# Attention's product of masked weights with values, computed in two halves of the array's columns

## The chip, the cores and the metric

The kernel runs on one core of one Trainium2 chip. The metric is the device time of one execution in microseconds (us), the median of several runs. One execution was also recorded by the hardware profiler; every row below is of that execution.

The core has a matrix engine (TensorE, PE in rows; its weight loads are listed apart as PEld), a vector engine (VectorE, DVE), a scalar engine (ScalarE, ACT), GpSimd (POOL) and SyncE (SP), which starts DMA transfers. A product on TensorE first loads one operand, the weights, into the 128 x 128 array, then streams the other operand, the moving columns, through it; the result lands in PSUM, one partition for each weight column.

## The reference

The program is an mLSTM attention followed by two mixture layers.

```
# attention, for every batch b (4), head h (8), step t (768), head width 40
C = f_stab * C + i_stab * outer(v_t, k_t)
n = f_stab * n + i_stab * k_t
y_t = sigmoid(o_t) * (C @ q_t) / max(|n . q_t|, 1)
# first layer: x is y with heads side by side, 3072 rows x 320
x = prelu(x @ w_in, alpha) @ w_out            # 320 -> 2048 -> 320
# second layer: each row goes to the one expert of 8 with the largest logit
out[row] = gate[row] * (relu(x[row] @ w1[e]) @ w2[e])
```

## The kernel before

The recurrence is computed in blocks of 128 steps. There are U = 24 units, one for each batch and block of 128 steps, and each unit does all 8 heads. For one unit:

- `att_s` (L762): scores of keys against queries, tiles `ps`. The contraction has only 40 rows, so two heads stand at once in the array, one on its rows 0 to 39 and one on rows 64 to 103.
- `att_e` and `att_m` (L752, L753, L770): the decay matrix `D` (steps by steps, one for each head) is loaded, exponentiated on ScalarE, masked on GpSimd, and multiplied with the scores on VectorE. D then holds the masked weights.
- `att_b` (L858): the product of D with the values, tile `pa`. For each head the weights are the 128 x 128 matrix D, the moving operand is 41 columns (40 of the values and one of ones, which gives the denominator). The products of 8 heads land side by side in one PSUM bank.
- `att_h`, `att_n`, `att_a` (L784, L805, L874): the part that comes from the state carried over from earlier blocks, tile `pb`, added to pa.
- `att_d` (L815), `att_u`, `att_v`: the block's contribution to the state, tile `pd`.
- `att_y` (L883 to L900), `att_c`, `att_x` (L911 to L923): division by the denominator, output gate, transposition (`pt`) into the first layer's input.

The first layer runs on 8 groups of 3 units. For each group and each of 16 slices of the hidden width there is `ffn1` (L934, tile `ph`, 8 products of 384 moving columns), an activation on ScalarE and VectorE (L947 to L956) and `ffn2` (L968 to L971, tiles `acc`, 9 products). The second layer (L326) runs after it, slot by slot. Weights of the first layer are also unpacked at the start (L658 to L662, L674, L691, L699, L712), and the experts' weights are split into two parts and written back to memory beside the first layer (L1206, L1207, L1214, L1215).

The order of all steps of the first part is written out by hand, in a list of step names (`ORDER`); `ab` is `att_b`, `as` is `att_s`, `F` is `ffn1`, `S` is `ffn2`. Each engine runs its instructions in that order. So blocks of attention products stand between the blocks of the first layer on TensorE.

An fp32 product appears in the trace as two rows of loads and two of matmuls; a product of the type fp32r (`ph`, `acc`, L326) as one. The tiles ps, pa, pb, pd, pt and some others share three PSUM banks by turns (`ps_att`).

Of the kernel before, what the change touches and what calls it, by code (L numbers as in the profile page):

```python
# [18 lines left out]
B, H, S, D = 4, 8, 768, 40  # L19
# [199 lines left out]
def mlstm_moe_kernel(  # L219
# [19 lines left out]
    V, A, G, T = nc.vector, nc.scalar, nc.gpsimd, nc.tensor  # L239
# [5 lines left out]
    def ps_att(name):  # L245
        return ps.tile([P, 512], F32, tag="att", bufs=3, name=name)
# [237 lines left out]
    with ExitStack() as p1:  # L484
# [367 lines left out]
        def att_b(u):  # L852
            b, c = divmod(u, NC)
            t = ut[u]
            v1 = t["kv"][:, 360:729]
            pa = ps_att(f"pa_{u}")
            for h in range(H):
                T.matmul(  # L858
                    pa[:, h * 41 : (h + 1) * 41],
                    t["D", h // 4][:, h % 4],  # L860
                    v1[:, h * 41 : (h + 1) * 41],
                    start=True,
                    stop=True,
                )
            t["pa0"] = pa

        def att_a(u):
# [566 lines left out]
```

## Time and profile before

| | |
|---|---|
| median of 3 runs | 764.89 us (762.24 to 766.14) |
| the profiled execution, its own time | 763.64 us |
| its span, first to last instruction | 761.8 us |
| TensorE matmuls, busy | 744.0 us (98%), 4907 rows |
| TensorE weight loads, busy | 711.0 us (93%) |
| VectorE, busy | 464.7 us (61%) |
| ScalarE, busy | 367.1 us (48%) |
| GpSimd, busy | 182.6 us (24%) |
| DMA | 179.38 MB in packets, mean 235 GB/s |

Busy shares are averages over a program with several stages. Matmuls are pipelined and the ends of their rows are modelled, so that neighbouring rows overlap; starts are measured. What a block on TensorE costs is therefore read from the start of its first row to the start of the next block's first row.

### The profile page before, as it was taken

Reading aid. Unit: us, or ns where it says so; the run is one execution under the profiler, and the core shown is the slowest. Engines: PE = TensorE matmul, PEld = TensorE weight load, DVE = VectorE, ACT = ScalarE, POOL = GpSimd, SP = SyncE. Lnnn points to the kernel's source line nnn. Section 1 sums busy time; section 2 is a strip of 40 time slices with the busy share of each in tenths; the row PEclk is TensorE's granted clock in tenths of the full one; section 3 lists DMA queues with packets and bytes.
Section 4 is the critical chain, followed back from the end, with each engine's and each line's share of the span. In section 5 each row is a group of like instructions: output and inputs, shape, how many; then the busy total and the mean of one; then the engine's idle time right before and its main releaser. Section 6 shows DMA issues by size and latency. Waiting matters only on the chain.

```text
span 761.8 us, 15188 instructions
## 1 busy us (share of the span) xinstructions
PE 744.0 (98%) x4907; PEld 711.0 (93%) x4907; DVE 464.7 (61%) x1119; ACT 367.1 (48%) x840; POOL 182.6 (24%) x240
## 2 busy tenths in 40 slices
PE   5999999999999999999999999999999999999997
PEld 5898999999999999999999999998999999999996
DVE  5888997867675576776787785867322232233222
ACT  3746586736655564654655454433333333233322
POOL 2443454423222232200010000013222232222223
PEclk9569999999999999999999999999999999999999
DMA  7876679879787848778787978794968645921100
GB/s 244 268 211 217 193 233 317 258 241 305 263 302 233 284 178 256 229 245 289 264 272 253 292 254 302 262 356 154 419 273 317 235 164 197 426 100 39 39 13 22
DMA packets 81515, 179.38 MB, mean 235 GB/s; under 512 B 8620, under 2 KB 39209, under 8 KB 80156
## 3 DMA queue, kind: packets, MB, share of 16 engines
q1 hardware_dynamic: 77980, 169.66, 65.0%
q0 software_dynamic: 3456, 8.71, 3.4%
q8 instruction: 45, 0.74, 0.4%
q14 instruction: 34, 0.28, 0.1%
HBM read 246.29 MB, written 55.59 MB: 396 GB/s over the span
## 4 chain that ended last, share of the span: by engine, by line
PE 85%; DVE 7%; DMA 2%; ACT 2%; issue 2%; POOL 1%; SPq 0%; POOLq 0%; ACTq 0%; DVEq 0%
PE ph L934 22%; PE po L326 13%; PE p L326 13%; PE acc L968 7%; PE acc L969 7%; PE acc L971 7%; PE pa L858 4%; PE p L424 3%; PE ps L762 3%; PE pb L784 1%; PE pd L815 1%; PE xt L386 1%; PE pt L911 1%; ACT D L752 1%; DMA er<-in_ew_dram 1%
## 5 line engine op out<-in xcount | busy, mean ns | idle before, releaser
L934 PE MATMUL ph<-ring 128*128 128x384 f32 x1024 | 198.3, 342 | 0.1
L934 PEld LDWEIGHTS ph<-ring 128*128 128x128 f32 x1024 | 177.7, 189 | 2.6 <-DVE ring L956 0.8
L968 PE MATMUL acc<-ring 128*128 128x336 f32 x384 | 122.4, 324 | 0.0
L969 PE MATMUL acc<-ring 128*128 128x336 f32 x384 | 119.5, 317 | 0.0
L947 ACT ACTIVATE v<-ph 128x384 f32<-128x384 f32 x128 | 62.4, 489 | 100.9 <-PE ph L934 98.7
L446 DVE TENSOR_SCALAR yo<-po,xg 128x320 f32<-128x320 f32 x26 | 14.3, 551 | 137.5 <-PE po L326 137.5
L326 PE MATMUL po<-ring,hh 128*128 (+1 forms) x432 | 95.6, 308 | 0.0
L949 DVE SCALAR_TENSOR_TENSOR ph<-v,al,ph 128x384 f32<-128x384 f32 x104 | 63.8, 618 | 49.3 <-ACT v L947 48.9
L326 PE MATMUL p<-ring,xh 128*128 (+1 forms) x324 | 89.9, 399 | 0.0
L971 PE MATMUL acc<-ring 128*128 128x336 f32 x384 | 80.1, 316 | 0.0
L326 PEld LDWEIGHTS po<-ring,hh 128*128 128x128 f32 x432 | 73.2, 187 | 2.3 <-ACT hh L426 0.2
L956 DVE TENSOR_TENSOR ring<-ph,ring 128x384 fp32r<-128x384 f32 x104 | 57.4, 554 | 27.0 <-ACT ring L955 26.1
L968 PEld LDWEIGHTS acc<-ring 128*128 128x128 f32 x384 | 72.2, 188 | 0.9
L969 PEld LDWEIGHTS acc<-ring 128*128 128x128 f32 x384 | 72.2, 188 | 0.0
L955 ACT ACTIVATE ring<-ph 128x384 fp32r<-128x384 f32 x104 | 50.6, 488 | 44.1 <-DVE ph L949 38.7
L426 ACT ACTIVATE hh<-p 128x512 fp32r<-128x512 f32 x54 | 29.4, 595 | 86.4 <-PE p L424 86.4
L326 PEld LDWEIGHTS p<-ring,xh 128*128 128x128 f32 x324 | 58.8, 188 | 11.5 <-DMA ring<-scr 0.2
L326 PE MATMUL po<-ring,hl 128*128 (+1 forms) x216 | 66.6, 308 | 0.2 <-DVE hl L428 0.2
L447 POOL DMA_INDIRECT out_dram<-yo,tok x28 | 28.1, 1003 | 160.8 <-DVE yo L446 135.8
L413 ACT ACTIVATE hr<-p 128x512 f32<-128x512 f32 x56 | 33.4, 597 | 67.5 <-PE p L326 65.1
L971 PEld LDWEIGHTS acc<-ring 128*128 128x128 f32 x384 | 63.6, 189 | 0.0
L752 ACT ACTIVATE D<-D,EKT 128x128 f32<-128x128 f32 x192 | 60.2, 393 | 3.5 <-DMA D<-gd 3.3
(211 smaller groups left out, 1180.4 us busy)
## 6 DMA issues: line engine op xcount, KB each, us to landing
ring<-scr SPq DMA_DIRECT2D x26, 3072.0 KB
ring<-scr SPq DMA_DIRECT2D x26, 2560.0 KB
ring<-scr SPq DMA_DIRECT2D x33, 512.0 KB
D<-gd SPq DMA_DIRECT2D x48, 256.0 KB
er<-in_ew_dram SPq DMA_DIRECT2D x32, 384.0 KB
scr<-ring SPq DMA_DIRECT2D x32, 384.0 KB
scr<-er SPq DMA_DIRECT2D x32, 384.0 KB
er<-in_ew_dram SPq DMA_DIRECT2D x32, 320.0 KB
```

The costliest lines, as they stand in the source:

```text
L326: mm = T.matmul(o_, lhsT, r, start=start, stop=stop)
L413: A.activation(hr_half(j, hf), ph, AF.Relu)
L752: A.activation(d[:, j], d[:, j], AF.Exp, bias=EKT[:, c, i + j : i + j + 1])
L858: T.matmul(pa[:, h * 41 : (h + 1) * 41], t["D", h // 4][:, h % 4], v1[:, h * 41 : (h + 1) * 41], start=True, stop=True,)
L934: T.matmul(ph[:, :384], wi_[i][lo][:, wc], xTs[n % 2][:, xc], start=(a == 0), stop=(a == len(PASSES) - 1),)
L947: A.activation(v, ph[:, :384], AF.Relu, scale=-1.0)
L949: V.scalar_tensor_tensor(g, v, al1[:, i : i + 1], ph[:, :384], ALU.mult, ALU.add)
L955: A.activation(gh, v, AF.Copy)
L956: engine(V, G, "ffn_split", k).tensor_tensor(gl, v, gh.bitcast(F32), ALU.subtract)
L968: T.matmul(ac, gh[:, sl], hi, start=(i == 0), stop=False)
L969: T.matmul(ac, gh[:, sl], lo, start=False, stop=False)
L971: T.matmul(accs[n][t][:, :NO], gl[:, t * P : (t + 1) * P], hi, start=False, stop=(i == NFC - 1))
```

## The change

In `att_b` each head's product is computed as two: the weights are columns 0 to 63 of D for the first and 64 to 127 for the second, and the results land in PSUM partitions 0 to 63 and 64 to 127 of the same tile and the same columns. In the built program the first has array position (row 0, column 0), the second (row 0, column 64), and both a size of 128 x 64, where it was one product of size 128 x 128 at position (0, 0). The products of L762 have size 64 x 128 at the positions (0, 0) and (64, 0), before as now. The moving operand, the values, is the same for both halves.

```diff
             pa = ps_att(f"pa_{u}")
             for h in range(H):
-                T.matmul(
-                    pa[:, h * 41 : (h + 1) * 41],
-                    t["D", h // 4][:, h % 4],
-                    v1[:, h * 41 : (h + 1) * 41],
-                    start=True,
-                    stop=True,
-                )
+                hs = slice(h * 41, (h + 1) * 41)
+                for hf in range(2):
+                    ts = slice(64 * hf, 64 * hf + 64)
+                    T.matmul(pa[ts, hs], t["D", h // 4][:, h % 4, ts], v1[:, hs], start=True, stop=True)
             t["pa0"] = pa
```

No instruction changes its place among the others. On TensorE, for the unit 11 that the rows below show, the order was (tile written, tiles read, size of the result in partitions x columns, and how many of the kind):

```order
L934 MATMUL ph_2495<-ring 128x384 x8
L858 MATMUL pa_2509<-kv_11_2340,D_0_2151 128x41 x4
L858 MATMUL pa_2509<-kv_11_2340,D_1_2319 128x41 x4
L934 MATMUL ph_2519<-ring 128x384 x8
L815 MATMUL pd_2535<-kv_12_2422,kt 120x123 x3
```

and with the change, on TensorE at the same place (lines behind the edit are lower by 3):

```order
L931 MATMUL ph_2583<-ring 128x384 x8
L861 MATMUL pa_2597<-kv_11_2428,D_0_2231 64x41 x8
L861 MATMUL pa_2597<-kv_11_2428,D_1_2399 64x41 x8
L931 MATMUL ph_2615<-ring 128x384 x8
L815 MATMUL pd_2631<-kv_12_2510,kt 120x123 x3
```

Eight products of 128 partitions have become sixteen of 64, with the halves of one head next to each other; their neighbours are the same.

## Rows read from the trace of the kernel before

**Rows 1.** The page: the span, and busy time of each engine.

```profile
span 761.8 us, 15188 instructions
PE 744.0 (98%) x4907; PEld 711.0 (93%) x4907; DVE 464.7 (61%) x1119; ACT 367.1 (48%) x840; POOL 182.6 (24%) x240
```

**Rows 2.** Stretches: length, busy time of each engine (rows), granted clock, DMA share, GB/s.

```profile
53.00:83.00 30.00, 28.04 (x207) 26.45 (x205) 25.72 (x57) 19.94 (x55) 10.74 (x13) 1.00 0.72 224
83.00:452.00 369.00, 368.77 (x2598) 361.54 (x2599) 272.75 (x642) 215.91 (x511) 87.16 (x123) 1.00 0.78 258
```

**Rows 3.** Waits of the weight loads, 83 to 452: in total, times, longest.

```profile
PEld ps L762 <- issue: 2.9, 13, 0.3
PEld ph L934 <- DVE ring L956: 0.8, 3, 0.4
```

**Rows 4.** The chain: shares of 22 to 83, and pieces (start, length) of 377 to 402.

```profile
by line: issue 10.9%; DMA er<-in_ew_dram 10.0%; DVE f_wi L662 7.4%; DVE f_wo L660 6.4%; DVE D L770 5.6%; DVE f_wo L662 5.5%; DVE f_wi L660 5.1%; DVE f_wo L658 4.1%; DVE state L850 3.8%; DVE f_wi L658 2.7%; DVE v L949 2.7%; PE ph L934 2.3%; 
...
385.19 4.10 DMA scr<-ring
...
391.05 6.10 DMA D<-gd
...
401.26 0.80 PE ph L934 x3
```

**Rows 5.** Stretches, instructions on pa alone: PE, PEld, DVE, ACT, then as before.

```profile
22.00:53.00 31.00, 8.56 (x41) 8.49 (x40) 3.46 (x11) 0.00 (x0) 0.50 0.76 235
83.00:452.00 369.00, 37.72 (x320) 37.97 (x320) 23.34 (x73) 1.58 (x8) 1.00 0.78 258
```

**Rows 6.** Timeline of TensorE around pa: start, length, instructions.

```profile
204.48 1.73 PE L934 MATMUL ph<-ring 128*128 128x384 f32 x9
206.05 1.87 PE L858 MATMUL pa<-kv,D 128*128 128x41 f32 x16
207.75 1.66 PE L934 MATMUL ph<-ring 128*128 128x384 f32 x8
209.24 0.48 PE L815 MATMUL pd<-kv,kt 128*120 128x123 f32 x3
...
384.20 1.88 PE L858 MATMUL pa<-kv,D 128*128 128x41 f32 x16
```

**Rows 7.** Timeline of the weight loads: a ps block, a pa block.

```profile
195.47 0.97 PEld L762 LDWEIGHTS ps<-q 40*128 40x128 f32 x16 [0.24 <-issue]
...
426.14 1.87 PEld L858 LDWEIGHTS pa<-kv,D 128*128 128x128 f32 x16
```

**Rows 8.** Groups of weight loads by line, a block each: busy time, mean ns of one.

```profile
L762 PEld LDWEIGHTS ps<-q 40*128 40x128 f32 x16 | 1.0, 187 | 0.2 <-issue 0.2
...
L858 PEld LDWEIGHTS pa<-kv,D 128*128 128x128 f32 x16 | 1.9, 192 | 0.0
...
L712 PEld LDWEIGHTS pwg<-wgt,woT 128*128 128x128 f32 x6 | 1.4, 334 | 0.0
...
L622 PEld LDWEIGHTS pe_dec<-gin,gcon 96*120 96x120 f32 x6 | 1.3, 321 | 0.0
...
L1092 PEld LDWEIGHTS <-bh 128*128 128x128 f16 x21 | 0.6, 96 | 0.2 <-issue 0.2
```

**Rows 9.** Timeline of the weight loads, early: 128 columns, and 120.

```profile
9.48 1.40 PEld L712 LDWEIGHTS pwg<-wgt,woT 128*128 128x128 f32 x6
...
13.62 1.32 PEld L622 LDWEIGHTS pe_dec<-gin,gcon 96*120 96x120 f32 x6
```

**Rows 10.** Timeline of TensorE around a ps block.

```profile
193.99 1.56 PE L934 MATMUL ph<-ring 128*128 128x384 f32 x8
195.47 1.16 PE L762 MATMUL ps<-q 40*128 40x128 f32 x16
196.56 1.68 PE L934 MATMUL ph<-ring 128*128 128x384 f32 x8
198.09 0.49 PE L911 MATMUL pt<-cst,y 128*128 128x128 f32 x3
```

## The prediction

> **What bounds the kernel now.** I read the page's first box, then the stretches, then the waits of the weight loads, then the chain that ended last, and last single stretches of the timeline around the edited line. TensorE is busy nearly all of the 761.8 us [rows 1]. A busy matmul row overlaps its neighbours, so that alone proves little. The stretches say where it counts. From 83 to 452 us the matmul rows cover 368.77 of 369 us, at a granted clock of 1.00, with VectorE at 272.75 and DMA at 0.78 [rows 2]. In those 369 us the largest wait of the weight loads for another engine is 0.8 us in total, at ph; the 2.9 us called "issue" are something else, used below [rows 3]. So between 83 and 452 us a microsecond of TensorE's own time is a microsecond of the kernel. Before 83 us this does not hold: the chain from 22 to 83 us goes through VectorE's decoding of the weights (L658 to L662), its state and D operations and a DMA, and TensorE's largest entry is ph with 2.3% [rows 4].
>
> The edited product writes tile pa. Of its 384 matmul rows (24 units, 8 heads, two rows for one fp32 product) 320 lie between 83 and 452 us: 20 units of 16 rows [rows 5]. The other four units lie before 83 us, most of their rows within 22 to 53 us, where the granted clock is 0.50, the lower of the two levels [rows 5]; I count nothing for these four.
>
> One stretch is an exception. From 377 to 401 us the chain leaves TensorE and runs through ScalarE, a 4.10 us DMA and a 6.10 us DMA, and comes back at 401.26 [rows 4]. The unit that starts at 384.20 lies beside it [rows 6], so its gain is not counted: 19 units.
>
> **What one unit costs now.** Between two ph blocks, pa starts at 206.05 and the next ph at 207.75: 1.70 us [rows 6]. The blocks abut: nine ph rows from 204.48 to 206.05 are 0.174 each, the pace inside a ph block, so entering pa costs nothing. Inside, the 16 weight loads set the pace: 16 of them take 1.87 us and one alone 0.192, so they follow each other every (1.87 - 0.19) / 15 = 0.112 us [rows 7, 8]. The moving side has only 41 columns.
>
> **What the change does to it.** Each head becomes two products, weight columns 0 to 63 and 64 to 127, on array columns 0 to 63 and 64 to 127; 16 rows a unit become 32, in 16 pairs. Nothing else moves; the order of blocks stays, and the consumers (L874, L883) find the same tile.
>
> *The step of a pair.* No row of before has a 64-column load or two column positions at work. The nearest is ps (L762), which already pairs products, there on two halves of the array's rows: its 16 loads of 128 columns take 0.97 us, one alone 0.187, so a pair takes (0.97 - 0.19) / 7 = 0.111 us [rows 7, 8], as much as one single load in pa. Two loads thus run side by side when they sit on different rows. Does a load cost by its columns? In the early rows, six 128-column loads follow every (1.40 - 0.33) / 5 = 0.214 us, six 120-column loads every (1.32 - 0.32) / 5 = 0.200 [rows 8, 9]; the pace there is slower than later, so only the ratio counts: 0.93, as 120 / 128 = 0.94. So I halve 0.112 to 0.056 and add 0.002 for a part that may not shrink: 0.058 us. The lower bound is how fast load and matmul rows can follow at all: the loads of 21 fp16 products in a row take 0.6 us, so (0.6 - 0.10) / 20 = 0.025 us each [rows 8], so 0.050 for a pair. The moving columns do not bind: ps streams 128 of them a row within 0.111 us, so 41 take at most 0.036. The upper bound is no pairing at all, 0.116, twice 0.058. I take 0.058, since loads, matmuls and both halves are laid out as in ps, with columns for rows.
>
> *Entering and leaving.* ps shows what changing the array's layout costs. Eight ph rows at 0.174 from 193.99 would end at 195.38; ps starts at 195.47, so 0.09 to enter [rows 10] (these are the "issue" gaps of [rows 3]). The ps block then lasts 1.09 us [rows 10]; eight steps of 0.111 are 0.89, so 0.20 goes to starting and draining. The ph block behind it takes 1.53 us (196.56 to 198.09) against 1.49 behind pa (207.75 to 209.24): up to 0.04, of which I take 0.03 [rows 6, 10]. In all 0.32 us a unit, which pa does not pay now.
>
> *Sum.* 16 x 0.058 + 0.32 = 1.25 us, against 1.70: 0.45 saved. Over 19 units that is 8.6 us. I take off 0.6 for stretches in which VectorE or a transfer, now about 2% closer, ends a wait last: 8.0 us. The profiled execution took 763.64 us, 1.25 below the median 764.89 of the runs shown; 763.64 - 8.0 = 755.6, and the same from the median is 756.9. I say 756.5.
>
> Its own bounds: at the floor of 0.050 and 20 units, 20 x (1.70 - 1.12) = 11.6 us; at a step of 0.066 and 18 units, 18 x (1.70 - 1.38) = 5.8, less 1 for absorbed gains, 4.8. From the median that is 753 to 760.
>
> **A rule that speaks against it.** In pa the 16 loads, all on the whole array's rows, follow each other every 0.112 us while each lasts 0.19 and matmuls are under way [rows 7, 8]: loads on the same rows do overlap matmuls there. The Trainium skill, page "TensorE: Matmul & The Clock Gate", section "Part 3: Packing small matmuls", says that a weight load overlaps matmuls in flight only where the row groups differ; the two halves here share all rows. Taken strictly that rule would deny the pairing and give the first rival below; the trace of pa does not bear it out for the whole array, and no run here shows column halves. The same section reports a speedup of 2.38 for three column tiles, at 512 moving columns, where loads weigh little.
>
> **The rivals.**
>
> *Loads one after the other (slower).* The two halves share rows, ps's halves don't. If a load of one half must wait for that of the other, a unit is 32 x 0.058 + 0.32 = 2.18 us: 0.48 more than now, x 19 = 9 us, 774. Nearly the same comes out if loads pair but 64 columns cost what 128 do: 16 x 0.112 + 0.32 = 2.11, 7.8 us, 772.7; the loads of 120 columns speak against that [rows 9]. It decides from a pair step of (1.70 - 0.32) / 16 = 0.086 us on. For it: nothing in the trace shows two loads on the same rows side by side. Chance 0.20.
>
> *A drain at every pair.* If half of the array's columns can't be reloaded while the other half streams, each pair pays the 0.20 of ps's ends: 16 x 0.258 + 0.12 = 4.25 us, 2.5 x 19 = 48 us, 813. Against it: within ps no pair pays it. Chance 0.08.
>
> *It isn't paired but costs no layout change either:* 32 loads of 64 columns back to back, 1.86 us, +0.16 x 19 = 3 us, 768. Against it: the products carry different array positions, as ps's do, so a change of layout is expected. Chance 0.04.
>
> *TensorE is no longer the bound.* The chain of 377 to 401 us shows that the path through ScalarE and the D transfers is close behind at one place [rows 4]; were it close everywhere, or were the clock to stay at 0.50 beyond 53 us because TensorE has less to do there (10 us more would cost 5 us of its work, against 2 us idle in the 30 us from 53 to 83 [rows 2]), the gain would shrink to 0 to 3 us: 762 to 765. Chance 0.08. Against it: the small waits [rows 3], and VectorE at 74% of 83 to 452 us.
>
> **How the numbers follow.** The forecast, 753 to 760 us, has 0.60. A change of 0.5%, 3.8 us, is about what can be told from none. Faster by more: 0.60 and a little of the shrunken gain, 0.62. Within: the unpaired case and most of the shrunken gain, 0.10. Slower: the serial loads and the drain, 0.28. To hold 8 in 10 the range must reach into the serial case: 753 to 774. Only the drain lies wholly outside.
>
> **What would show it.** Right: a pa block between ph blocks lasts about 1.13 us instead of 1.70, its 32 loads stand in pairs a few ns apart and 0.05 to 0.06 us from pair to pair, "issue" waits of about 0.2 us stand ahead of pa loads, and 83 to 452 shrinks by 8 us with TensorE still busy throughout. Wrong: loads evenly spaced 0.058 us apart (serial), steps of 0.11 (column count doesn't matter), or gaps of 0.2 inside the block (drain). If the block shrinks as said and the span doesn't, the waits of the weight loads for D, ring or y must have grown by as much.

## The result and the profile after

The changed kernel takes 755.84 us (median of 4 runs, 755.59 to 756.81); the kernel before takes 763.81 us in the runs beside it (4 runs, 762.24 to 766.14). The ratio is 0.9896, with a 95% interval of 0.9865 to 0.9926: faster by 0.7 to 1.4%. The forecast was 756.5 us. The profiled execution took 756.81 us.

The page, as [rows 1]; there are 384 more rows on TensorE, and all of them are pa's:

```profile
span 755.0 us, 15956 instructions
PE 734.8 (97%) x5291; PEld 693.3 (92%) x5291; DVE 463.7 (61%) x1119; ACT 367.6 (49%) x840; POOL 183.6 (24%) x240
```

The timeline of TensorE at the unit of [rows 6] and at another:

```profile
202.78 1.73 PE L931 MATMUL ph<-ring 128*128 128x384 f32 x9
204.44 1.13 PE L861 MATMUL pa<-kv,D 128*64 128x41 f32 x32
205.54 1.68 PE L931 MATMUL ph<-ring 128*128 128x384 f32 x8
207.06 0.48 PE L815 MATMUL pd<-kv,kt 128*120 128x123 f32 x3
...
249.84 1.13 PE L861 MATMUL pa<-kv,D 128*64 128x41 f32 x32
250.91 0.42 PE L965 MATMUL acc<-ring 128*128 128x336 f32 x1
```

From a block's first row to the next block's first row it is 1.10 and 1.07 us; the median over the 20 blocks from unit 4 to unit 23 is 1.063, where before it is 1.704. Nine ph rows at 0.174 from 202.78 would end at 204.35, so entering costs 0.09. The ph block behind takes 1.52 us where it took 1.49 [rows 6]; the first row of the block behind pa loses 0.02 to 0.03.

The weight loads of that block: first how many loads of pa begin up to 204.455, 204.495 and 204.51 us (count, shortest, median and longest in ns), then the block as one row of the timeline:

```profile
L861 PEld LDWEIGHTS pa<-kv,D x2: 133/133/133, 204.4 to 204.4; 128*64 128x64 f32 x2
...
L861 PEld LDWEIGHTS pa<-kv,D x2: 133/133/133, 204.4 to 204.4; 128*64 128x64 f32 x2
...
L861 PEld LDWEIGHTS pa<-kv,D x4: 133/134/136, 204.4 to 204.5; 128*64 128x64 f32 x4
...
204.44 1.01 PEld L861 LDWEIGHTS pa<-kv,D 128*64 128x64 f32 x32 [0.25 <-issue]
```

Two loads begin within the first 0.015 us, none in the next 0.04, then two more: the halves load in pairs, the second 6 to 7 ns behind the first, each lasting about 0.136. With 0.138 for the last load, the step from pair to pair is (1.01 - 0.14) / 15 = 0.058 us. The wait of 0.25 called "issue" stands ahead of the block.

To see what became of the time, I compare one stretch of the program in all kernels: from the first pa row of unit 4 to the first pa row of unit 23, which holds 19 pa blocks. The starts differ between executions by up to 6 us (84.8 to 90.8), because of the part ahead of them that TensorE does not bound; behind the stretch all have 312 to 314 us left. Stretches (length, then PE, PEld, DVE, ACT and POOL busy, granted clock, DMA share, GB/s), of the kernel before:

```profile
87.40:448.20 360.80, 360.73 (x2544) 353.50 (x2543) 265.29 (x625) 211.60 (x502) 86.25 (x122) 1.00 0.79 259
```

and of the changed one:

```profile
88.78:441.96 353.18, 351.43 (x2847) 338.46 (x2846) 264.09 (x624) 212.15 (x502) 86.87 (x122) 1.00 0.80 265
```

It is shorter by 7.6 us. TensorE, which had 0.07 us without a matmul row, now has 1.75. The blocks give more than 7.6: 19 x (1.704 - 1.063 - 0.09 - 0.02) = 10.1, the 0.09 for entering and 0.02 for a slower start of the block behind. So 2.5 us are lost again. The loss isn't spread over the units: from one pa block to the next, twelve of the 19 distances fall by 0.49 to 0.66 us, as the sum for a block says, and seven (behind units 5, 6, 9, 14, 17, 18 and 20) by nothing to 0.34. The waits of the weight loads, 83 to 452, as [rows 3], show what TensorE waits for:

```profile
PEld ph L931 <- DVE ring L953: 2.9, 8, 0.7
PEld ps L762 <- issue: 2.9, 13, 0.3
PEld pa L861 <- issue: 2.5, 11, 0.3
PEld pwg L712 <- DVE ring L719: 1.6, 1, 1.6
PEld acc L965 <- ACT ring L952: 0.6, 1, 0.6
PEld pt L908 <- DVE D L770: 0.5, 1, 0.5
```

The wait of ph for VectorE's L953 (L956 before) was 0.8 us and is 2.9. The 1.6 of L712 ends at 82.9 us, ahead of the stretch.

### The profile page after: what moved, and what is told of

It is laid out like the page before. It is cut to its first block, busy times and chain, and to the rows that moved or that the text cites. A ratio compares the mean times of both kernels' runs of the same rounds, so it can differ in the third digit from the quotient of the medians.

```text
span 755.0 us, 15956 instructions
## 1 busy us (share of the span) xinstructions
PE 734.8 (97%) x5291; PEld 693.3 (92%) x5291; DVE 463.7 (61%) x1119; ACT 367.6 (49%) x840; POOL 183.6 (24%) x240
## 4 chain that ended last, share of the span: by engine, by line
PE 79%; DVE 6%; ACT 2%; DMA 2%; issue 1%; POOL 0%; SPq 0%; POOLq 0%; DVEq 0%; ACTq 0%
PE ph L931 20%; PE po L326 13%; PE p L326 13%; PE acc L965 7%; PE acc L966 6%; PE acc L968 6%; PE p L424 3%; PE ps L762 2%; PE pa L861 2%; PE pb L784 1%; DMA D<-gd 1%; PE pd L815 1%; PE xt L386 1%; DMA r_wi<-in_wi_dram 1%; PE pt L908 1%
## 5 line engine op out<-in xcount | busy, mean ns | idle before, releaser
L946 DVE SCALAR_TENSOR_TENSOR ph<-v,al,ph 128x384 f32<-128x384 f32 x104 | 63.8, 618 | 47.7 <-ACT v L944 47.2
L953 DVE TENSOR_TENSOR ring<-ph,ring 128x384 fp32r<-128x384 f32 x104 | 57.4, 555 | 26.1 <-ACT ring L952 24.7
L952 ACT ACTIVATE ring<-ph 128x384 fp32r<-128x384 f32 x104 | 50.6, 489 | 43.7 <-DVE ph L946 38.9
```

The source lines that it names most:

```text
L946: V.scalar_tensor_tensor(g, v, al1[:, i : i + 1], ph[:, :384], ALU.mult, ALU.add)
L952: A.activation(gh, v, AF.Copy)
L953: engine(V, G, "ffn_split", k).tensor_tensor(gl, v, gh.bitcast(F32), ALU.subtract)
```

## The experiments

All but the last control are edits of the changed kernel, and all ratios are to the kernel before, run on the same chip.

**The halves apart.** All lower halves first, then all upper ones; the same 32 rows, with no two neighbours on different halves but in the middle.

```diff
-            for h in range(H):
-                hs = slice(h * 41, (h + 1) * 41)
-                for hf in range(2):
-                    ts = slice(64 * hf, 64 * hf + 64)
+            for hf in range(2):
+                ts = slice(64 * hf, 64 * hf + 64)
+                for h in range(H):
+                    hs = slice(h * 41, (h + 1) * 41)
                     T.matmul(pa[ts, hs], ...)
```

> All eight lower halves of a unit first, then all eight upper halves; the number of products and the two changes of layout stay. Side by side (two loads run at once only because the halves of one head are neighbours in the program): the 32 loads follow one another every 0.058 us, a pa block takes 32 x 0.058 + 0.2 = 2.1 us instead of 1.1, 20 units x 1.0 us lost against the changed kernel: about 774 to 776 us, slower than before the change. Narrow loads alone (a 64-column load is simply cheaper, neighbours don't matter): 756 us as the changed kernel. If TensorE reaches 32 instructions ahead to the other half, also near 756, and the trace would show lower and upper loads at the same moment.

Measured: 765.64 us (10 runs), ratio 1.0031 (1.0016 to 1.0046). The gain is gone, so narrower loads alone don't give it: it takes the pairing. The loss is smaller than expected (774 to 776 us). TensorE's timeline, then how many of the block's loads had begun by 204.9, 205.2, 205.4 and 206.1 us:

```profile
204.48 1.85 PE L861 MATMUL pa<-kv,D 128*64 128x41 f32 x32
206.26 0.44 PE L931 MATMUL ph<-ring 128*128 128x384 f32 x1
...
L861 PEld LDWEIGHTS pa<-kv,D x8: 133/138/138, 204.5 to 204.9; 128*64 128x64 f32 x8
...
L861 PEld LDWEIGHTS pa<-kv,D x13: 133/138/138, 204.5 to 205.2; 128*64 128x64 f32 x13
...
L861 PEld LDWEIGHTS pa<-kv,D x20: 133/138/138, 204.5 to 205.4; 128*64 128x64 f32 x20
...
L861 PEld LDWEIGHTS pa<-kv,D x32: 133/138/138, 204.5 to 206.1; 128*64 128x64 f32 x32
```

From 204.9 to 205.2 five loads begin, one every 0.06 us, the serial pace. From 205.2 to 205.4, where the program goes from the 16 lower rows to the upper ones, seven begin, twice that pace, and from there on 12 in 0.7 us again. I read the middle as the last three or four lower rows with the first upper ones beside them, though they aren't neighbours in the program. So the block is 1.78 us, where 32 x 0.058 and 0.13 for its end would be 1.99. Against before, the blocks and their entries cost 19 x (0.08 + 0.09 + 0.02) = 3.6 us; the stretch from unit 4 to 23 is 363.20, 2.4 longer than before. The 1.2 between the two I did not trace.

**Quarters.** Four products of 32 columns a head.

```diff
-                for hf in range(2):
-                    ts = slice(64 * hf, 64 * hf + 64)
+                for hf in range(4):
+                    ts = slice(32 * hf, 32 * hf + 32)
```

> Four products of 32 weight columns a head instead of two of 64. Side by side with a floor of 0.025 us a row, as the 21 fp16 products of before show it: 64 rows in 16 steps of 4 x 0.025 = 0.10 us or more, a block of 1.6 + 0.2 = 1.8 us against 1.1: 20 x 0.7 = 14 us lost, about 769 us, slower than before the change. If only the load's columns set the step (0.03 us for 32): a block of 16 x 0.03 + 0.2 = 0.7 us, 8 us gained, 748 us.

Measured: 751.35 us (4 runs, 750.74 to 751.52), ratio 0.9843 (0.9817 to 0.9868): faster than both kernels. The timeline of TensorE and of the weight loads, the waits of the loads in 83 to 452, and the rows of the block from 200.617 us that had begun by 200.64:

```profile
246.44 0.82 PE L861 MATMUL pa<-kv,D 128*32 128x41 f32 x64
247.19 0.42 PE L965 MATMUL acc<-ring 128*128 128x336 f32 x1
...
200.62 0.69 PEld L861 LDWEIGHTS pa<-kv,D 128*32 128x32 f32 x64 [0.25 <-issue]
...
PEld ph L931 <- DVE ring L953: 5.9, 12, 1.0
...
PEld pt L908 <- DVE D L770: 1.1, 1, 1.1
...
L861 PE MATMUL pa<-kv,D x4: 224/224/224, 200.6 to 200.6; 128*32 128x41 f32 x4
```

The block lasts 0.75 us, and the step of four is (0.69 - 0.11) / 15 = 0.039 us, a load lasting 0.11. The expectation of 769 took the 0.025 us between the fp16 loads of [rows 8] as a floor for every row of the engine, 0.100 for four; four rows in 0.039 refute that for rows on different column positions. The first four rows of a block begin 6 to 7 ns apart. Further on the positions drift out of step, and starts lie 0 to 34 ns apart, at about the same mean pace.

**Where the gain arises.** Halves in the first four units alone, then in the other twenty alone (`u >= 4`).

```diff
+            n = 2 if u < 4 else 1
...
-                for hf in range(2):
-                    ts = slice(64 * hf, 64 * hf + 64)
+                for hf in range(n):
+                    ts = slice(P // n * hf, P // n * (hf + 1))
```

> Halves only in units 0 to 3, which lie before 83 us; units 4 to 23 as before. TensorE bound from 83 us on: no change against before, 764 us, within 1 us. Gain from elsewhere (the stretch from 22 to 53 us, whose granted clock was 0.50 in the profile of before and 1.00 in that of the changed kernel): all of the 8 us, 756 us.

> Halves only in units 4 to 23; units 0 to 3 as before. TensorE bound from 83 us on: all of the gain, 756 us. Gain from elsewhere: 764 us, as before. A share between the two would say that both count.

Measured: 763.51 us for the first four (12 runs), ratio 1.0001 (0.9986 to 1.0016); 756.08 for the last twenty (6 runs), ratio 0.9908 (0.9881 to 0.9934). The first four give nothing, the other twenty all of it. The stretches from unit 4 to 23 say the same: 360.75 us with the first four (before: 360.80), 354.19 with the last twenty (after: 353.18).

**pb in halves too.** On top of the change, L784 is split in the same way: six rows of 128 weight columns and 123 moving columns become twelve in pairs.

```diff
+                    gs = slice(gq * 123, (gq + 1) * 123)
+                    for hf in range(2):
+                        ts = slice(64 * hf, 64 * hf + 64)
+                        T.matmul(pb[ts, gs], t["qg"][:, gq, ts], state[:, gs], start=True, stop=True)
```

> On top of the change, the product of L784 (tile pb, 123 moving columns, three products a unit, 20 units) is split into halves in the same way. Side by side, but a step lasts at least as long as its moving columns stream: 123 of them take about 0.105 us a row, as pd's rows show, so 6 pairs take 6 x 0.107 instead of 6 x 0.112, and two changes of layout are added, 0.25 us a unit: 17 units behind 83 us lose 0.2 each, of which about three quarters reach the end: 758 to 759 us, against 756 of the changed kernel. If halving the loads were what counts whatever streams: pairs of 0.058, 0.1 us a unit gained, 754 to 755 us.

Measured: 757.49 us (6 runs), ratio 0.9927 (0.9903 to 0.9950), an interval that overlaps that of the change alone. The trace is clearer. A pb block of the changed kernel:

```profile
178.70 0.83 PE L784 MATMUL pb<-state,qg 120*128 120x123 f32 x6
179.29 1.65 PE L931 MATMUL ph<-ring 128*128 128x384 f32 x8
```

and the same block in halves:

```profile
176.64 0.86 PE L787 MATMUL pb<-state,qg 120*64 120x123 f32 x12
177.42 1.67 PE L928 MATMUL ph<-ring 128*128 128x384 f32 x8
```

0.59 us became 0.78, and the stretch from unit 4 to 23 is 356.04 us, 2.9 more than with the change alone. Whole, the rows of pb start every 0.111 us, the pace of a 128-column load; in halves a pair costs (0.78 - 0.13) / 6 = 0.108, where 0.13 is the end of a pa block (worked out below). So half the load hardly shortened the step, and the block paid for the layout besides; what set that step the next two kernels tell. The rows of pd, from which the expectation took 0.105 for 123 columns, could not show it by themselves: their loads have 120 columns, and 0.112 x 120 / 128 is 0.105 as well.

**Twice the moving columns.** Halves, then quarters, with 82 moving columns in place of 41; the second 41 fall on the next head's place and are written over by its product.

```diff
-                hs = slice(h * 41, (h + 1) * 41)
+                hs = slice(h * 41, (h + 2) * 41)
```

> The changed kernel with 82 moving columns instead of 41 in pa; the second 41 are overwritten by the next head's product. Two halves side by side, each step the longer of load and stream: 82 columns need twice the time of 41. If 41 take 0.034 us (two passes of a column a row, at 2.4 GHz) plus 0.004 for the row, 82 take 0.073, above the load's 0.058: a block of 16 x 0.073, 0.23 us more, 20 units, three quarters of it: 759 us. If the two halves shared one stream: steps of 0.14, 20 x 1.3, 776 us or more. If the load set the step whatever streams: 756 us.

> Quarters with 82 moving columns. If in the quarters' run the 0.039 us from step to step were the 41 moving columns (0.034 and 0.004), the step is 0.073 here, the same as with halves of 82 columns: block and time as in that run, near 759 us. If 0.039 were four rows of about 0.01 us to issue, it stays 0.039: 751 us.

Measured: 757.02 us for the halves (4 runs), ratio 0.9912 (0.9878 to 0.9947), and 756.64 for the quarters (4 runs), ratio 0.9919 (0.9887 to 0.9951). Both are below the 759 expected, and the times alone do not part the halves of 82 columns from those of 41. The blocks do; TensorE's timeline with halves:

```profile
189.38 1.36 PE L861 MATMUL pa<-kv,D 128*64 128x82 f32 x32
190.67 0.42 PE L965 MATMUL acc<-ring 128*128 128x336 f32 x1
```

and with quarters:

```profile
186.86 1.34 PE L861 MATMUL pa<-kv,D 128*32 128x82 f32 x64
188.13 0.42 PE L965 MATMUL acc<-ring 128*128 128x336 f32 x1
```

With 82 moving columns halves and quarters take nearly the same 1.29 and 1.27 us, or (1.29 - 0.13) / 16 = 0.073 us a step; with 41 they take 1.06 and 0.75. So at 82 the moving columns set the step and at 41, in halves, the load does. From 82 to pb's 123 columns the step grows from 0.073 to 0.108, some 0.85 ns a column; 41 columns less than 82 gives 0.038, close to the step of the quarters. That the columns set the step there too is read off this line; no run had fewer than 41. The step is then the larger of two times: the load of one position (0.112 us for 128 columns, 0.058 for 64) and the moving columns (0.038 us for 41, 0.073 for 82, 0.108 for 123). In pb the columns already took nearly as long as the load, so halving the load bought next to nothing and the change of layout was paid.

**Who takes back part of the gain.** In quarters, and in the kernel before as a control, the slices of the first layer from 24 on go without VectorE's alpha term (L946, 0.62 us each).

```diff
-            V.scalar_tensor_tensor(g, v, al1[:, i : i + 1], ph[:, :384], ALU.mult, ALU.add)
+            if k < KEEP:
+                V.scalar_tensor_tensor(g, v, al1[:, i : i + 1], ph[:, :384], ALU.mult, ALU.add)
```

> The quarters' kernel without VectorE's part of the first layer's activation from slice 24 on (the alpha term is left out; ScalarE's part still runs and is not used): ph goes to the split as it is, so its PSUM buffer comes free about 0.6 us earlier and VectorE has 104 x 0.62 us less to do. To be read from the start of the pa block of unit 4 to that of unit 23: 360.8 us before, 353.2 with halves, 350.7 with quarters, while 19 blocks shrank by 16 us with quarters. Lost to waits of ph for VectorE's release of its buffer: those waits (5.9 us with quarters) all but vanish and the stretch comes to 345 to 346. Lost elsewhere (DMA, the D chain, the clock): it stays within 1 us of 350.7, less what the next run gains.

> The kernel before with the same piece of work left out, as a control for the run with quarters: the waits of ph were 0.8 us there, so the stretch from unit 4 to unit 23 should fall by no more than 1 us, from 360.8 to 359.8 or so. If it falls by 5 us, that piece of work binds for another reason and the other run says nothing on the quarters.

Measured: 749.65 us for the quarters (2 runs), ratio 0.9807 (0.9735 to 0.9880), and 762.76 for the control (8 runs), ratio 0.9990 (0.9964 to 1.0016). The values that reach the second layer differ, so I read only the stretch from unit 4 to 23. Quarters as they are:

```profile
85.35:436.04 350.69, 346.00 (x3456) 332.39 (x3455) 264.02 (x626) 211.99 (x502) 86.51 (x122) 1.00 0.81 267
```

quarters without the term, and their largest wait on VectorE in 83 to 452:

```profile
87.56:434.12 346.56, 344.33 (x3455) 332.55 (x3454) 220.16 (x546) 210.27 (x503) 88.35 (x123) 1.00 0.81 270
...
PEld ph L931 <- DVE ring L954: 1.6, 3, 0.8
```

the kernel before without the term:

```profile
90.80:450.68 359.88, 359.88 (x2543) 353.50 (x2543) 221.05 (x546) 209.48 (x504) 87.29 (x123) 1.00 0.78 260
```

Less work on VectorE is worth 350.69 - 346.56 = 4.1 us (about 5 was expected) beside short pa blocks and 360.80 - 359.88 = 0.9 beside long ones. Each stretch is from one execution, and kernels that are the same in it differ by up to 1.0 us (353.18 and 354.19 above). VectorE's busy share in the stretch is 75% in the quarters; it isn't full, it is late at certain places.

## Why the prediction was right

**The step of a pair** was the decisive choice: 0.058 us from ps's pairs and halved loads; measured 0.058. The loads stand in pairs a few ns apart, as the prediction said they would if it were right. The serial rival falls with that (the halves apart show what serial loads give), as do the drain at every pair (no gap inside the block), the full price for 64 columns, and the unpaired case.

**The rule that spoke against it.** Loads on the same rows of the array, on different columns, run side by side: two loads of 0.136 us each begin 7 ns apart, and a pair takes 0.058. The rule of the Trainium skill, page "TensorE: Matmul & The Clock Gate", section "Part 3: Packing small matmuls", by which a load overlaps matmuls in flight only where the row groups differ, does not hold for column halves here, where the serial loads that would follow from it do not appear.

**Entering and leaving** was over-sized. Entering, 0.09, came as in ps. Start and drain were put at 0.20 from ps; a pa block has 1.063 - 16 x 0.0585 = 0.13. The next block lost 0.02 at most places, not 0.03. In all 0.24 instead of 0.32 us a unit, so a unit saves 0.53 and not 0.45, and 19 of them 10.1 us, not 8.6.

**The absorbed part** was under-sized: 0.6 us was taken off, with no row behind that number; 2.5 was measured (3.5 by the kernel with halves in the last twenty units, which is the same in this stretch). The prediction named the sign to look for, grown waits of the loads, but put its price too low. One place shows the mechanism. TensorE before, in the stretch of a pa block, a transposition and a ph block:

```profile
265.69 1.87 PE L858 MATMUL pa<-kv,D 128*128 128x41 f32 x16
267.39 0.52 PE L911 MATMUL pt<-cst,y 128*128 128x128 f32 x3
267.67 1.67 PE L934 MATMUL ph<-ring 128*128 128x384 f32 x8
```

The same place after, TensorE, then VectorE:

```profile
262.55 1.13 PE L861 MATMUL pa<-kv,D 128*64 128x41 f32 x32
263.61 0.55 PE L908 MATMUL pt<-cst,y 128*128 128x128 f32 x3
264.44 0.45 PE L931 MATMUL ph<-ring 128*128 128x384 f32 x1 [0.29 <-DVE ring L953]
...
262.25 0.49 DVE L896 TENSOR_TENSOR y<-y,so 128x320 f32<-128x320 f32 x1
262.66 1.20 DVE L946 SCALAR_TENSOR_TENSOR ph<-v,al,ph 128x384 f32<-128x384 f32 x2
263.83 1.15 DVE L953 TENSOR_TENSOR ring<-ph,ring 128x384 fp32r<-128x384 f32 x2
```

in quarters (two rows), and in quarters without the alpha term (three rows), TensorE:

```profile
258.82 0.82 PE L861 MATMUL pa<-kv,D 128*32 128x41 f32 x64
...
260.73 0.44 PE L931 MATMUL ph<-ring 128*128 128x384 f32 x1 [0.62 <-DVE ring L953]
...
258.92 0.82 PE L861 MATMUL pa<-kv,D 128*32 128x41 f32 x64
259.67 0.55 PE L908 MATMUL pt<-cst,y 128*128 128x128 f32 x3
260.61 1.68 PE L931 MATMUL ph<-ring 128*128 128x384 f32 x8 [0.39 <-DVE ring L954]
```

The tiles ph share two PSUM buffers, and the next ph must wait until VectorE's L953 has read the older one. Before, ph began 1.98 us after pa, with no wait: the long pa block covered VectorE's four operations on the two older ph tiles. After, pa is 0.64 us shorter and ph still begins only 1.89 us after it, when the first L953 is done. Here the gain of the block is all but lost. In quarters ph begins 1.91 us after pa, no earlier, and without the alpha term 1.69. The experiment with its control shows that more than half of the quarters' loss hangs on VectorE's work: they lost 19 x (1.704 - 0.749 - 0.11) - (360.80 - 350.69) = 5.9 us, and 3.2 us more comes back in them (4.1 less 0.9) than in the kernel before. That the remainder is made up of the waits for L770, L952 and the transfers is likely from the list of waits, but was not tested.

**The sum** came out right because the two errors have opposite signs: 10.1 - 2.5 = 7.6 us in the stretch, against 8.6 - 0.6 = 8.0: that they cancel is luck. The medians are 763.81 - 755.84 = 7.97 us apart; such agreement is finer than the scatter of the runs. The count of 19 units was not tested by itself. The stretch has 19 blocks too, but others: the excluded unit is among them and unit 23 is not. The block of the excluded unit shrank as the others did. From it to the next pa block the changed kernel gained 0.27 us, but the kernel with halves in the first four units alone, in which that unit is as before, gained 0.43, so these traces don't tell what that unit gave. The first four units were shown to give nothing.

**The clock staying low** did not come about: from unit 4 on the granted clock is 1.00 in both kernels, and between 53 and 752 us the half level is recorded after the change only from 83.4 to 86.8 us. The kernel with halves in the last twenty units, which up to there is the kernel before, has it too, from 82.7 to 86.2, so the shorter blocks are not needed for it. But the 0.50 of [rows 5] for 22 to 53 us needs care. The same stretch of pa after the change, and a block of an early unit:

```profile
22.00:53.00 31.00, 4.51 (x72) 3.91 (x70) 3.46 (x11) 0.00 (x0) 1.00 0.77 229
...
40.63 1.94 PE L861 MATMUL pa<-kv,D 128*64 128x41 f32 x32
```

The clock column now says 1.00, yet this block takes 1.94 us where later ones take 1.13: the pace of the slower level (with pb in halves the same block takes 1.94 us as well, at a recorded 0.50). The clock's records begin at 18.7 us in the profile before and at 52.6 us in the one after; ahead of the first record the column says nothing, and the duration of a known block says more.

**What is better than both:** quarters, 751.35 us. They were only tried for pa. From the step above I take them to be near the end of this road: at 0.039 the moving columns seem to bind, and more than a third of the blocks' gain (5.9 of 16.1 us) is already lost again, over half of that to VectorE.

## What to carry to other kernels

For fp32 products as measured here, splitting a product's weight columns over column positions pays where its load takes longer than its moving columns: the step falls to the larger of (load / number of positions) and the columns' time, and each block pays about 0.24 us for the change of layout; where columns already take nearly as long as the load, as in pb, it costs. Put the parts of one product next to each other in the program, and before pricing the gain look at which engine used the long block as cover: with two buffers between TensorE and VectorE, part of what TensorE saves returns as its wait for the buffer.

## What the runs showed of the hardware that was not expected

- Rows on different column positions can start 6 to 7 ns apart, and four of them take 0.039 us, while rows on one position were never nearer than 0.025 us in the rows read here.
- Loads of parts that are not neighbours in the program pair up to some extent: with the halves apart, seven loads begin in 0.2 us in the middle of the block, where the serial pace gives three or four.
- An fp32 row's time follows its moving columns at some 0.85 ns each (82 to 123 columns: 0.073 to 0.108 us), about as much as a weight column of a load (0.112 us for 128: 0.88 ns).
